# Norms of the first layer's weights over pairs of pieces, and four features at a time in one-tile chunks

## The chip, the cores and the metric

The kernel runs on one core of one Trainium2 chip. The metric is the device time of one execution in microseconds (us), lower is better. The engines are TensorE (PE, with its weight loads PEld), VectorE (DVE), ScalarE (ACT), GpSimd (POOL) and SyncE (SP), which issues the DMA transfers.

## What is computed

Attention within clusters, then two feed-forward layers. B = 2, H = 8 heads, S = 768, D = 64; 16 clusters; model width 512, hidden width 2048.

```
q_assign, k_assign = argmax over the centroids of the normalised q and k
mask  = q_assign[:, :, :, None] == k_assign[:, :, None, :]
x     = softmax(where(mask, q @ k.T / sqrt(D), -1e9)) @ v     # to (1536, 512)
h     = x @ moe_w_in;   x = (h * sigmoid(h)) @ moe_w_out      # first layer
h     = x @ moe2_w_in
out   = (max(h, 0) + alpha * min(h, 0)) @ moe2_w_out          # second layer
```

## The kernel before, in words

All data is fp32 and every product is made of three fp16 products: an operand x is scaled by a power of two and split into a high and a low fp16 part, and high x high, high x low and low x high are added in PSUM.

The tokens are 12 tiles of 128. Attention goes tile by tile and, in a tile, head by head; one head of one tile is a unit. `front` (L786) makes its scores on PE (L796, L800), the scaling and the maximum on DVE (L810), the exponential and its high part on ACT (L815, L819) and its low part on DVE (L820); a transposing DMA (L826) turns the result and `back` (L828) multiplies it with v (L838). When the eight heads of a tile are done, `x_done` (L851) scales and splits the tile of x and a DMA transposes it.

The first layer, `layer1` (L1158), takes tiles in chunks, `CHUNKS` (L22): chunks 0 and 1 have one tile each (n = 128 columns), the other five have two (n = 256). For each of the KF = 16 blocks of 128 hidden features it makes 12 matmuls (L1190). Two blocks share one PSUM tile `hp` of 2 x n columns, taken from the two banks `w` in turn (the function `psum`, L469). Then come four elementwise instructions over both blocks: tanh on ACT (L1197), a product on DVE (L1198), the high part on ACT (L1201) and the low part on DVE (L1202). The scale of tanh is a column of `dh`, which in chunk 0 is made one column at a time (L1180) as the scales of the weights arrive. After that, 4 output blocks of 48 matmuls each (L1221), evacuated by ACT (L1228).

The weights come as fp32 words in pieces of 128 x 1024: 8 pieces of `moe_w_in` (`in_tasks`, L958) and 8 of `moe_w_out` (`out_tasks`, L1008). A piece is loaded (L892), converted by ACT (L903, L907) and DVE (L914, L917), and its sum of squares is taken by `sum_sq_pe` (L946): 8 matmuls of 128 x 128 blocks of the piece with themselves, added in a `w` bank (L952), and one DVE instruction that takes the diagonal and adds it up (L954, with an accumulator read). `scale` (L981) sums over a pair of pieces and over the partitions with matmuls against ones (`all_sum`, L503), makes a power of two (`pow2_scale`: L445 and L447 on DVE, L450 and L453 on POOL) and splits both pieces (L929 on ACT, L930 on DVE); then the buffers of the pair are loaded again. Both columns of a pair get the same scale. For `moe_w_out` one scale over all 8 pieces is made (L1033) and the pieces are split after it. These functions serve the second layer's weights too; there (`w2`) the sum of squares is an ACT instruction (L944).

The program's order is not the order on the engines. `plan_order` (L313) gives all instructions a cost from a table in the code (`costs`, L75), finds their dependences, and lays them out on the engines' queues by a list schedule: once in program order, then 60 times backward and forward with priorities that carry Gaussian noise (`improve`, L193). The order with the earliest modelled end of all of these is then forced on the queues of PE, DVE, ACT, POOL and SP. Which PSUM bank a tile gets is fixed before, by the program's order.

Of the kernel before, what the change touches and what calls it, by code (L numbers as in the profile page):

```python
# [11 lines left out]
F32 = mybir.dt.float32  # L12
# [34 lines left out]
class Plan:  # L47
# [144 lines left out]

    def improve(self, rounds):  # L193

        noise = Random(1)
        found = [self.run(list(range(len(self.ins))))]
        back = self.mirror()
        for _ in range(rounds):
            back.run([noise.gauss(0, 0.1) - t for t in self.ended])
            found.append(self.run([noise.gauss(0, 0.1) - t for t in back.ended]))  # L200
        return min(found, key=lambda x: x[0])
# [128 lines left out]
def cluster_attention_silu_prelu(  # L330
# [20 lines left out]
    nc = tc.nc  # L351
# [25 lines left out]
    def view(off, dt, *dims):  # L377
        n = 1
        for d in dims:
            n *= d  # L380
        nb = n * (2 if dt in (F16, BF16) else 4)
        assert off % 4 == 0 and nb % 4 == 0 and off + nb <= total, (off, nb)
        a = arena[:, off // 4:(off + nb) // 4]
        if dt != F32:
            a = a.bitcast(dt)
        if len(dims) == 1:
            return a
        names = [f"a{i}" for i in range(len(dims))]
        pat = f"p ({' '.join(names)}) -> p {' '.join(names)}"
        return a.rearrange(pat, **{n: d for n, d in zip(names, dims)})  # L390
# [103 lines left out]
    def all_sum(cols, kind="m"):  # L494

        if not isinstance(cols[0], list):
            cols = [cols]
        n = cols[0][0].shape[1]
        ps = psum(kind, n * len(cols))
        for q, line in enumerate(cols):  # L500
            for i, c in enumerate(line):
                top = c.bitcast(BF16).rearrange("p (n t) -> p n t", t=2)[:, :, 1]
                nc.tensor.matmul(  # L503
                    out=ps[:, q * n:(q + 1) * n], lhsT=ones, rhs=top, start=(i == 0), stop=(i == len(line) - 1)
                )
        return ps
# [436 lines left out]

        nc.scalar.activation(out=junk, in_=t, func=ACTF.Square, accum_out=ss)  # L944

    def sum_sq_pe(tb, ss, kind):  # L946


        ps = psum(kind, 128)
        for i in range(PC // 128):  # L950
            c = tb[:, i * 128:(i + 1) * 128]
            nc.tensor.matmul(out=ps, lhsT=c, rhs=c, start=(i == 0), stop=(i == PC // 128 - 1))  # L952
        junk = view(o_junk, BF16, 128)
        nc.vector.scalar_tensor_tensor(  # L954
            out=junk, in0=ps, scalar=1.02, in1=ident, op0=ALU.mult, op1=ALU.mult, accum_out=ss
        )

    def in_tasks(w, raws, o_dst, kind, modes, mp):  # L958

        m = Weight()  # L960
        m.s, m.inv, ss = col(NPC), col(NPC), col(NPC)
        m.smin, m.inv_smin = col(1), col(1)
        tasks = []

        def raw(j):
            return view(raws[j % len(raws)], I32, PC, 2)

        def load(j):
            if j < NPC:
                n = w.shape[0] // 2  # L970
                return load_piece(w[j % 2 * n:(j % 2 + 1) * n, j // 2 * 2 * FW:(j // 2 + 1) * 2 * FW], raw(j))

        def conv(j):
            t = raw(j)[:, :, 1].bitcast(F32)
            to_f32(raw(j), t, mp[j])
            if w2:
                sum_sq(t, raw(j)[:, :, 0].bitcast(F32), ss[:, j:j + 1])
            else:
                sum_sq_pe(view(raws[j % len(raws)], BF16, PC, 4)[:, :, 3], ss[:, j:j + 1], kind)

        def scale(b):  # L981
            if not w2:
                for o in range(8 * b, 8 * b + 8):
                    assert o < 8 or (("k", 0, (o - 8) // 3) if o < 20 else ("v", 0, (o - 20) // 3)) in did
            both = range(2 * b, 2 * b + 2)
            tot = all_sum([[ss[:, j:j + 1] for j in both]] * 2, kind)
            pow2_scale(tot, 2, 14 if w2 else 15, None, m.s[:, both[0]:both[0] + 2], m.inv[:, both[0]:both[0] + 2])
            for j in both:
                d = view(o_dst + 8 * KB * b, F16, 2, 2, PC)[:, :, j % 2]
                t = raw(j)[:, :, 1].bitcast(F32)  # L990
                split(t, d[:, 0], d[:, 1], m.s[:, j:j + 1], modes[j])
            for j in both:
                load(j + len(raws))
            if b == NPC // 2 - 1:
                nc.vector.tensor_reduce(out=m.smin, in_=m.s, axis=AX.X, op=ALU.min)
                nc.vector.tensor_reduce(out=m.inv_smin, in_=m.inv, axis=AX.X, op=ALU.max)

        m.loads = [lambda j=j: load(j) for j in range(len(raws))]
        m.scales = [lambda b=b: scale(b) for b in range(NPC // 2)]
        for j in range(NPC + 1):  # L1000
            if j < NPC:
                tasks.append(lambda j=j: conv(j))
            if j and j % 2 == 0:
                tasks.append(m.scales[j // 2 - 1])
        m.tasks = tasks
        return m

    def out_tasks(w, raws, o_ts, o_dst, m_in, kind, modes, mp):  # L1008

        m = Weight()  # L1010
        s, m.inv, ss, rho = col(1), col(1), col(NPC), col(NPC)

        def raw(j):
            return view(raws[j % len(raws)], I32, PC, 2)

        def load(j):
            if j < NPC:
                n = w.shape[0] // NPC
                load_piece(w[j * n:(j + 1) * n], raw(j))

        def conv(j):
            if not w2 and j < 6:
                for o in range(4 * j, 4 * j + 4):
                    assert ("k", 0, o // 6) in did
            t = view(o_ts[j], F32, PC)
            to_f32(raw(j), t, mp[j])
            if w2:
                sum_sq(t, raw(j)[:, :, 0].bitcast(F32), ss[:, j:j + 1])
            load(j + len(raws))
            if not w2:  # L1030
                sum_sq_pe(view(o_ts[j], BF16, PC, 2)[:, :, 1], ss[:, j:j + 1], kind)

        def scale():  # L1033
            tot = all_sum([ss[:, j:j + 1] for j in range(NPC)], kind)
            pow2_scale(tot, 1, 15, None, s, m.inv)
            nc.vector.tensor_scalar(rho, m_in.inv, m_in.smin, s, op0=ALU.mult, op1=ALU.mult)

        def piece(j):
            d = out_piece(o_dst, j)
            split(view(o_ts[j], F32, 2, DM), d[:, 0], d[:, 1], rho[:, j:j + 1], modes[j])  # L1040

        m.loads = [lambda j=j: load(j) for j in range(len(raws))]
        m.tasks = [lambda j=j: conv(j) for j in range(NPC)]
        m.scale = scale
        m.late = [lambda j=j: piece(j) for j in range(NPC)]
        return m
# [111 lines left out]
    def layer1(c):  # L1158
# [14 lines left out]
        first = t0 % T == 0  # L1173
        if c and first:
            nc.vector.tensor_scalar(dh, w1["in"].inv, x_inv[b], 0.5, op0=ALU.mult, op1=ALU.mult)
        for f in range(KF):
            j = f // 2
            wi = [in_block(o_w, f // 2 * 2 + ff) for ff in range(2)]
            if c == 0 and f % 2 == 0:
                nc.vector.tensor_scalar(  # L1180
                    dh[:, j:j + 1], w1["in"].inv[:, j:j + 1], x_inv[b], 0.5,
                    op0=ALU.mult, op1=ALU.mult,
                )
            if f % 2:
                hp = psum("l", 2, n)
                for ff in range(2):
                    i = 0
                    for kd in range(KD):
                        for a, bb in ((0, 0), (0, 1), (1, 0)):
                            nc.tensor.matmul(  # L1190
                                out=hp[:, ff], lhsT=wi[ff][:, a, kd],
                                rhs=mov(bb, kd), start=(i == 0), stop=(i == 3 * KD - 1),
                            )
                            i += 1
                th = view(o_tmp + 2 * KB * ring("t1", 2), F32, 2, n)
                gh, gl = g[:, f - 1:f + 1, 0], g[:, f - 1:f + 1, 1]
                nc.scalar.activation(out=th, in_=hp, func=ACTF.Tanh, scale=dh[:, j:j + 1])  # L1197
                nc.vector.scalar_tensor_tensor(  # L1198
                    out=th, in0=th, scalar=1.0, in1=hp, op0=ALU.add, op1=ALU.mult
                )  # L1200
                nc.scalar.activation(out=gh, in_=th, func=ACTF.Copy, scale=2.0 ** -16)  # L1201
                nc.vector.scalar_tensor_tensor(  # L1202
                    out=gl, in0=th, scalar=2.0 ** -16, in1=gh, op0=ALU.mult, op1=ALU.subtract,
                )
            yield
# [395 lines left out]
```

## Time and profile before

| what | value |
|---|---|
| median of 3 runs (lowest to highest) | 753.65 us (753.04 to 754.53) |
| the profiled execution: time, span | 756.6 us, 754.8 us |
| PE busy | 663.7 us (88%) |
| DVE busy | 598.3 us (79%) |
| ACT busy | 482.2 us (64%) |
| POOL busy | 128.7 us (17%) |
| mean granted clock of TensorE | 0.964 |

The span is the part of the profiled execution that the trace covers; all times of rows are in us from its start, if not marked ns. Busy shares are means over stages with different limits, so they say little by themselves; the rows below go by stretches.

### The profile page before, as it was taken

The numbers are of one execution on the slowest core, as the hardware profiler recorded it, in microseconds if no ns is written. First come the engines' busy times: TensorE is split into PE (matmuls) and PEld (weight loads), VectorE is DVE, ScalarE is ACT, GpSimd is POOL, SyncE is SP. The second block draws the span as 40 slices with busy tenths as digits, with TensorE's granted clock in tenths as the row PEclk, the third lists the DMA queues.
The fourth block names the chain that finished last, engine by engine and source line by source line (L and its number), as shares of the span: only waits on it lengthen the run. The fifth ranks groups of instructions, "written<-read, shape, count | busy, mean of one in ns | idle before, by whom it ended". The sixth has DMA issues, their size and how long they took to land.

```text
span 754.8 us, 17044 instructions
## 1 busy us (share of the span) xinstructions
PE 663.7 (88%) x7035; PEld 500.2 (66%) x7035; DVE 598.3 (79%) x1084; ACT 482.2 (64%) x779; POOL 128.7 (17%) x231
## 2 busy tenths in 40 slices
PE   0363568689999999999999999998899999999997
PEld 0243346579888888888888898874344677666643
DVE  4798998998888689858977856779899999966650
ACT  7886967978879568747866967878664442422111
POOL 4442021432234532102120020100000000000000
PEclk9995558999999999999999999999999999999999
DMA  7979998999999898888897932353300100001001
GB/s 230 307 196 288 331 216 132 172 196 172 195 181 209 147 168 137 135 153 146 149 152 124 279 76 97 129 199 140 112 1 0 56 2 1 1 1 56 1 0 56
DMA packets 237357, 100.86 MB, mean 134 GB/s; under 512 B 217312, under 2 KB 227552, under 8 KB 237280
## 3 DMA queue, kind: packets, MB, share of 16 engines
q1 hardware_dynamic: 237280, 99.78, 60.9%
q8 instruction: 55, 0.90, 0.5%
q14 instruction: 22, 0.18, 0.1%
HBM read 43.03 MB, written 3.15 MB: 61 GB/s over the span
## 4 chain that ended last, share of the span: by engine, by line
PE 46%; DVE 13%; DMA 6%; ACT 4%; issue 3%; POOL 2%; ACTq 0%; POOLq 0%
PE s L1477 11%; PE w L1190 10%; PE w L1221 9%; PE x L838 4%; PE w L1434 4%; DVE arena L930 3%; DMA arena<-in_moe_w_out_dram 3%; PE s L796 2%; PE s L800 2%; DMA arena<-in_moe_w_in_dram 2%; PE x L1434 2%; PE m L1434 2%; DVE arena L1300 1%; DVE arena L917 1%; DVE arena L914 1%
## 5 line engine op out<-in xcount | busy, mean ns | idle before, releaser
L1190 PE MATMUL w<-arena 128*128 128x256 f16 (+1 forms) x1272 | 152.7, 258 | 3.6 <-DMA arena<-arena 2.3
L1221 PE MATMUL w<-arena 128*128 128x256 f16 (+1 forms) x1296 | 154.1, 257 | 1.6 <-DVE arena L1198 1.1
L1477 PE MATMUL s<-arena 128*128 128x512 f16 x576 | 136.1, 379 | 1.4 <-DVE arena L930 1.4
L838 PE MATMUL x<-arena 128*128 128x64 f16 x1728 | 120.3, 196 | 7.3 <-DMA arena<-arena 7.3
L1190 PEld LDWEIGHTS <-arena 128*128 128x128 f16 x1344 | 109.7, 98 | 18.3 <-issue 6.7
L1221 PEld LDWEIGHTS <-arena 128*128 128x128 f16 x1344 | 110.2, 98 | 16.2 <-issue 2.1
L815 ACT ACTIVATE s<-s,stat 128x768 f32<-128x768 f32 x96 | 83.9, 873 | 56.0 <-DVE s L810 49.2
L810 DVE TENSOR_SCALAR_CACHE_REDUCE s<-s,stat 128x768 f32<-128x768 f32 x96 | 97.6, 1021 | 24.3 <-PE s L800 23.2
L838 PEld LDWEIGHTS <-arena 128*128 128x128 f16 x1728 | 97.5, 100 | 19.7 <-DMA arena<-arena 9.3
L820 DVE TENSOR_TENSOR arena<-s,arena 128x768 f16<-128x768 f32 x96 | 91.4, 953 | 13.0 <-ACT arena L819 12.6
L1477 PEld LDWEIGHTS <-arena 128*128 128x128 f16 x576 | 56.0, 98 | 61.1 <-issue 2.3
L796 PE MATMUL s<-arena 80*128 80x384 f16 x192 | 68.0, 354 | 12.6 <-DVE arena L820 11.1
L819 ACT ACTIVATE arena<-s 128x768 f16<-128x768 f32 x96 | 77.5, 809 | 1.7 <-DMA arena<-arena 0.3
L1434 PEld LDWEIGHTS <-arena 128*128 128x128 f16 x672 | 65.6, 98 | 17.3 <-issue 1.0
L1394 ACT ACTIVATE arena<-arena,stat 128x512 f16<-128x512 f32 x48 | 33.6, 717 | 66.1 <-DVE arena L1391 66.0
L800 PE MATMUL s<-arena 128*128 128x384 f16 x192 | 68.2, 355 | 0.0
L450 POOL TENSOR_SCALAR stat<-stat 128x1 int32<-128x1 int32 (+1 forms) x41 | 11.6, 286 | 307.0 <-DVE stat L445 210.1
L914 DVE SCALAR_TENSOR_TENSOR arena<-arena 128x1024 int32<-128x1024 int32 x32 | 39.1, 1222 | 22.6 <-ACT arena L907 22.4
L1434 PE MATMUL w<-arena 128*128 128x256 f16 x336 | 56.5, 273 | 0.0
L930 DVE SCALAR_TENSOR_TENSOR arena<-arena,stat 128x1024 f16<-128x1024 f32 x40 | 51.9, 1315 | 4.9 <-ACT arena L929 4.9
L903 ACT ACTIVATE arena<-arena 128x1024 int32<-128x1024 uint32 x32 | 37.0, 1155 | 26.8 <-DMA arena<-in_moe_w_in_dram 16.4
L929 ACT ACTIVATE arena<-arena,stat 128x1024 f16<-128x1024 f32 x40 | 45.7, 1171 | 11.7 <-POOL stat L450 4.4
(176 smaller groups left out, 1061.6 us busy)
## 6 DMA issues: line engine op xcount, KB each, us to landing
arena<-in_moe_w_in_dram SPq DMA_DIRECT2D x16, 1024.0 KB, 6.1
arena<-in_moe_w_out_dram SPq DMA_DIRECT2D x16, 1024.0 KB, 6.4
arena<-in_k_dram SPq DMA_DIRECT2D x8, 384.0 KB, 4.8
arena<-in_q_dram SPq DMA_DIRECT2D x6, 512.0 KB, 5.1
arena<-in_v_dram SPq DMA_DIRECT2D x8, 384.0 KB, 5.1
out_dram<-arena SPq DMA_DIRECT2D x12, 256.0 KB, 2.1
arena<-arena SPq DMA_TRANSPOSE x149, 4.2
arena<-in_centroids_dram SPq DMA_DIRECT2D x1, 32.0 KB, 2.9
```

The costliest lines, as they stand in the source:

```text
L796: nc.tensor.matmul(out=sc[:, j, :hs], lhsT=qt2[0:D + C, h], rhs=kt2[0:D + C, h % 2, j * hs:(j + 1) * hs], start=True, stop=False,)
L800: nc.tensor.matmul(out=sc[:, j, :hs], lhsT=qt1[:, h], rhs=kt1[:, h % 2, j * hs:(j + 1) * hs], start=False, stop=True,)
L810: nc.vector.tensor_scalar(sc[:, :, :hs], sc[:, :, :hs], nd_cols[:, H * (n % 2) + h:H * (n % 2) + h + 1], None, op0=ALU.mult, op1=ALU.min, ...
L815: nc.scalar.activation(out=p, in_=p, func=ACTF.Exp, scale=-1.0, bias=bias, accum_out=sums[n % 2][:, h:h + 1])
L819: nc.scalar.activation(out=hl[:, 0], in_=p, func=ACTF.Copy)
L820: nc.vector.tensor_tensor(out=hl[:, 1], in0=p, in1=hl[:, 0], op=ALU.subtract)
L838: nc.tensor.matmul(out=x_ps[0][:, h], lhsT=pt[:, ph * T + t], rhs=vt[:, h % 2, t, vh], start=(i == 0), stop=(i == 3 * T - 1),)
L930: nc.vector.scalar_tensor_tensor(out=lo, in0=t, scalar=s, in1=hi, op0=ALU.mult, op1=ALU.subtract)
L1190: nc.tensor.matmul(out=hp[:, ff], lhsT=wi[ff][:, a, kd], rhs=mov(bb, kd), start=(i == 0), stop=(i == 3 * KD - 1),)
L1221: nc.tensor.matmul(out=acc, lhsT=wo[:, a, f % 2, dt * 128:(dt + 1) * 128], rhs=g[:, f, bb], start=(i == 0), stop=(i == 3 * KF - 1),)
L1434: nc.tensor.matmul(out=hp[:, ff], lhsT=a_[:, a, kd, at + 128 * ff:at + 128 * ff + 128], rhs=b_[:, bb, kd], start=(k == 0), stop=(k == 5),)
L1477: nc.tensor.matmul(out=acc[t], lhsT=g[:, q, a, t * 128:(t + 1) * 128], rhs=wo[:, bb, f % 2], start=(first and q == 0 and k == 0), stop=(la ...
```

## The change

`sum_sq_pe` takes a list of pieces: for the first layer's weights it is called once for each pair of pieces, after the odd one, and adds 16 matmuls in one bank before one reduction on DVE. The sum of squares of a pair stands in the odd piece's column, and the sums over the partitions read the odd columns alone. In `layer1`, `nf = 512 // n` blocks of features share a PSUM tile: four in the one-tile chunks, two in the others as before; the four elementwise instructions then go over 4 x 128 columns. `dh` is made for two columns at a time. The planner's random numbers start from 4 in place of 1.

```diff
     def improve(self, rounds):
-        noise = Random(1)
+        noise = Random(4)
...
-    def sum_sq_pe(tb, ss, kind):
+    def sum_sq_pe(tbs, ss, kind):
         ps = psum(kind, 128)
-        for i in range(PC // 128):
-            c = tb[:, i * 128:(i + 1) * 128]
-            nc.tensor.matmul(out=ps, lhsT=c, rhs=c, start=(i == 0), stop=(i == PC // 128 - 1))
+        parts = [tb[:, i * 128:(i + 1) * 128] for tb in tbs for i in range(PC // 128)]
+        for i, c in enumerate(parts):
+            nc.tensor.matmul(out=ps, lhsT=c, rhs=c, start=(i == 0), stop=(i == len(parts) - 1))
...
# in_tasks
-            else:
-                sum_sq_pe(view(raws[j % len(raws)], BF16, PC, 4)[:, :, 3], ss[:, j:j + 1], kind)
+            elif j % 2:
+                sum_sq_pe(
+                    [view(raws[i % len(raws)], BF16, PC, 4)[:, :, 3] for i in (j - 1, j)],
+                    ss[:, j:j + 1], kind,
+                )
...
-            tot = all_sum([[ss[:, j:j + 1] for j in both]] * 2, kind)
+            tot = all_sum([[ss[:, j:j + 1] for j in (both if w2 else both[1:])]] * 2, kind)
...
# out_tasks
-            if not w2:
-                sum_sq_pe(view(o_ts[j], BF16, PC, 2)[:, :, 1], ss[:, j:j + 1], kind)
+            if not w2 and j % 2:
+                sum_sq_pe(
+                    [view(o_ts[i], BF16, PC, 2)[:, :, 1] for i in (j - 1, j)],
+                    ss[:, j:j + 1], kind,
+                )
...
-            tot = all_sum([ss[:, j:j + 1] for j in range(NPC)], kind)
+            tot = all_sum([ss[:, j:j + 1] for j in range(0 if w2 else 1, NPC, 1 if w2 else 2)], kind)
...
# layer1
+        nf = 512 // n
         for f in range(KF):
-            j = f // 2
-            wi = [in_block(o_w, f // 2 * 2 + ff) for ff in range(2)]
-            if c == 0 and f % 2 == 0:
+            j = f // 4 * 2
+            if c == 0 and f % 4 == 0:
                 nc.vector.tensor_scalar(
-                    dh[:, j:j + 1], w1["in"].inv[:, j:j + 1], x_inv[b], 0.5,
+                    dh[:, j:j + 2], w1["in"].inv[:, j:j + 2], x_inv[b], 0.5,
                     op0=ALU.mult, op1=ALU.mult,
                 )
-            if f % 2:
-                hp = psum("l", 2, n)
-                for ff in range(2):
+            if f % nf == nf - 1:
+                hp = psum("l", nf, n)
+                for ff in range(nf):
                     i = 0
+                    wi = in_block(o_w, f - nf + 1 + ff)
...
-                                out=hp[:, ff], lhsT=wi[ff][:, a, kd],
+                                out=hp[:, ff], lhsT=wi[:, a, kd],
...
-                th = view(o_tmp + 2 * KB * ring("t1", 2), F32, 2, n)
-                gh, gl = g[:, f - 1:f + 1, 0], g[:, f - 1:f + 1, 1]
+                th = view(o_tmp + 2 * KB * ring("t1", 2), F32, nf, n)
+                gh, gl = g[:, f - nf + 1:f + 1, 0], g[:, f - nf + 1:f + 1, 1]
```

## Rows read from the trace of the kernel before

**Rows 1.** Busy time by stretch; columns: stretch, length, engines, PE clock, DMA share, GB/s.

```profile
20.00:125.00 105.00, 56.71 (x628) 41.42 (x629) 92.91 (x191) 80.48 (x111) 30.84 (x46) 0.74 1.00 255
125.00:200.00 75.00, 65.35 (x1191) 57.13 (x1188) 69.85 (x147) 64.66 (x126) 19.77 (x31) 1.00 1.03 172
200.00:460.00 260.00, 259.19 (x3373) 224.48 (x3371) 196.40 (x387) 186.57 (x329) 61.98 (x96) 1.00 0.86 160
460.00:620.00 160.00, 151.23 (x1002) 95.64 (x1001) 144.47 (x187) 105.19 (x147) 6.21 (x22) 1.00 0.22 80
620.00:755.00 135.00, 129.82 (x826) 80.30 (x824) 84.76 (x138) 31.87 (x47) 0.34 (x2) 1.00 0.05 16
```

**Rows 2.** Instructions by line and form: min/median/max ns with first, last start; or busy, mean ns.

```profile
L954 DVE SCALAR_TENSOR_TENSOR arena<-w,arena x16: 273/282/292, 25.5 to 124.4; 128x128 bf16<-128x128 f32 x16
L954 DVE DVE_READ_ACCUMULATOR arena<-w,arena x16: 75/83/85, 25.7 to 124.6; 128x1 f32 x16
...
L1180 DVE TENSOR_SCALAR stat<-stat x8: 196/199/202, 103.8 to 105.9; 128x1 f32<-128x1 f32 x8
...
L1197 ACT ACTIVATE arena<-w,stat x16: 465/474/492, 123.9 to 196.2; 128x256 f32<-128x256 f32 x16
...
L1198 DVE SCALAR_TENSOR_TENSOR arena<-arena,w x16: 408/414/422, 126.0 to 198.3; 128x256 f32<-128x256 f32 x16
...
L1202 DVE SCALAR_TENSOR_TENSOR arena<-arena x16: 409/418/427, 128.0 to 200.5; 128x256 f16<-128x256 f32 x16
...
L1202 DVE SCALAR_TENSOR_TENSOR arena<-arena 128x512 f16<-128x512 f32 x40 | 29.5, 739 | 4.2 <-ACT arena L1201 4.1
...
L1197 ACT ACTIVATE arena<-w,stat 128x512 f32<-128x512 f32 x37 | 25.3, 684 | 5.7 <-PE w L1190 5.3 <-DVE arena L1202 0.2
L1198 DVE SCALAR_TENSOR_TENSOR arena<-arena,w 128x512 f32<-128x512 f32 x37 | 25.2, 682 | 3.0 <-ACT arena L1197 3.0
L1201 ACT ACTIVATE arena<-arena 128x512 f16<-128x512 f32 x40 | 24.9, 626 | 2.2 <-DVE arena L1198 1.9
...
L1201 ACT ACTIVATE arena<-arena 128x256 f16<-128x256 f32 x16 | 6.6, 414 | 1.5 <-DVE arena L1198 1.3
```

**Rows 3.** Timeline of DVE: start, duration (us), line, operation, shapes, count.

```profile
47.10 0.28 DVE L954 SCALAR_TENSOR_TENSOR arena<-w,arena 128x128 bf16<-128x128 f32 x1
...
47.31 1.22 DVE L917 SCALAR_TENSOR_TENSOR arena<-arena 128x1024 int32<-128x1024 int32 x1
...
103.81 0.56 DVE L1180 TENSOR_SCALAR stat<-stat 128x1 f32<-128x1 f32 x4
...
152.51 0.41 DVE L1198 SCALAR_TENSOR_TENSOR arena<-arena,w 128x256 f32<-128x256 f32 x1
152.85 0.42 DVE L1202 SCALAR_TENSOR_TENSOR arena<-arena 128x256 f16<-128x256 f32 x1
153.18 1.02 DVE L810 TENSOR_SCALAR_CACHE_REDUCE s<-s,stat 128x768 f32<-128x768 f32 x1
...
231.53 0.68 DVE L1198 SCALAR_TENSOR_TENSOR arena<-arena,w 128x512 f32<-128x512 f32 x1
232.13 0.68 DVE L1202 SCALAR_TENSOR_TENSOR arena<-arena 128x512 f16<-128x512 f32 x1
```

**Rows 4.** Waits from 20 to 125 us, then 125 to 200: total us, times, longest.

```profile
PE w L952 <- DVE arena L917: 14.0, 5, 5.6
PE w L952 <- DVE arena L954: 3.0, 3, 1.0
...
ACT arena L903 <- DMA arena<-in_moe_w_in_dram: 7.8, 3, 4.8
...
PE x L838 <- DMA arena<-arena: 5.2, 5, 2.5
PE w L1190 <- DVE arena L1198: 1.3, 3, 0.7
...
PE w L1221 <- DVE arena L1198: 1.1, 1, 1.1
```

## Prediction

> **What bounds the kernel now.** I read first the busy time of each engine by stretches of the span [rows 1]. There the reader is to see a change of limit. From 200 to 460 us TensorE (PE) is busy 259.2 of 260 us, and from 200 to the end it idles 0.8 + 8.8 + 5.2 = 14.8 us in all. So nothing done to VectorE (DVE) or ScalarE (ACT) there can give more than part of 14.8 us. Before 200 us PE is far from full: 56.7 of 105 us from 20 to 125, 65.4 of 75 from 125 to 200. In the same stretches DVE is busy 92.9 of 105 (88%) and 69.9 of 75 (93%), ACT 77% and 86%. The DMA engines show a share of 1.00 and 1.03. The early part is therefore carried by DVE, with transfers close behind, and whatever brings PE sooner to its full load moves everything after 200 us forward by the same amount.
>
> Second, the instructions of the lines that the diff touches, with their first and last start [rows 2]. All lie before 201 us: the 16 norm reductions (L954) from 25.5 to 124.4 us, the eight dh products from 103.8 to 105.9, the elementwise work of the two one-tile chunks from 123.9 (its first tanh, L1197) to 200.5. Third, the timeline of DVE [rows 3], for the distance from the start of one instruction to the start of the next, since durations overlap. Last, the waits in the two early stretches [rows 4].
>
> **The change, part by part.** The sum is made against the profiled execution: 756.6 us with a span of 754.8, so 1.8 us lie around the span. It is 2.95 us above the median of the three runs (753.65), and I take that off at the end.
>
> *Norms over pairs.* The number of norm matmuls (L952) stays at 128. Of the 16 reductions with their accumulator reads 8 go. By duration one is 0.282 + 0.083 us, together 8 x 0.365 = 2.9 us [rows 2]. In the timeline the next real instruction starts 0.21 us after the reduction (47.10 to 47.31) [rows 3], so DVE gets back 8 x 0.21 = 1.7 us. The sums over partitions (L503) lose 2 matmuls in each of 4 scales and 4 in the last: 12 one-column matmuls on a PE that idles half of that stretch, costed at nothing; were PE full there they would be a gain of some tenths. A norm group now opens with the even piece and closes with the odd one, so one of the two w banks is held from the first to the last of 16 matmuls. Before, a scale waited for the odd piece too, so the scale (L445, L450), the split (L929, L930) and the next weight load behind it get no later. PE's three waits of a norm for a reduction before it, 3.0 us [rows 4], go, since only one bank is now taken per pair; what is late next is the conversion itself (L917), for which PE waits 14.0 us [rows 4], so those 3.0 us count for nothing. If the order puts the even piece's matmuls too early, the score matmuls (L796, L800) queue behind them on PE; a DVE instruction needs those soon, and the longest of these waits is now 5.6 us [rows 4].
>
> *dh in four steps instead of eight.* Four in a row take 0.56 us with 0.199 for one [rows 2, 3], so (0.56 - 0.20)/3 = 0.12 us apart: 4 x 0.12 = 0.5 us saved. That a second column costs nothing is an assumption; the bound is the same price twice, which gives no saving.
>
> *Elementwise work over four features.* 16 instructions of 256 columns become 8 of 512 in each of four lines. L1198: the next instruction starts 0.34 us after the 256-column form (152.51 to 152.85) and 0.60 after the 512-column one (231.53 to 232.13) [rows 3]: 16 x 0.34 - 8 x 0.60 = 0.6. L1202: 0.33 us apart (152.85 to 153.18) for 256 columns; for 512 I take the same 0.60, as its duration in that place is L1198's 0.68 [rows 3]: 16 x 0.33 - 8 x 0.60 = 0.5. ACT by duration: L1197 16 x 0.474 - 8 x 0.684 = 2.1 and L1201 16 x 0.414 - 8 x 0.626 = 1.6 [rows 2]; ACT has 10 us free in 125 to 200 [rows 1], so its 3.7 us stand at nothing, covered by DVE; without that cover they would be a further gain.
>
> DVE's sum is 1.7 + 0.5 + 0.6 + 0.5 = 3.3 us, of which 2.2 lie before 125 us and 1.1 behind. Weighted with DVE's busy share (for in the rest of the time another thing ended the wait) 2.2 x 0.88 + 1.1 x 0.93 = 3.0 us.
>
> By full durations the same four terms are 2.9 + 0.8 + (16 x 0.414 - 8 x 0.682 = 1.2) + (16 x 0.418 - 8 x 0.739 = 0.8) = 5.7 us [rows 2]. In the timeline DVE's instructions start 0.07 to 0.09 us before the one ahead has ended [rows 3], so 3.3 is what I take, and 5.7 is an end of the range. The Trainium skill ("VectorE: DVE Perf Modes", The DRAIN you can't avoid) says that the next op does not start until the pipe is empty, with an exception for ops that are not held; by that rule the sum would be the 5.7. This trace speaks for the exception: its starts lie closer than its durations.
>
> *What it adds.* A 512-column group passes tanh and L1198 (0.684 + 0.682) in place of 0.474 + 0.414, so the last group of a chunk releases its bank and gives its g 0.48 us later. The output matmuls (L1221) already wait once, 1.1 us, for L1198 [rows 4], and nothing but attention's own matmuls lies behind them on PE. Two chunks x 0.48 is 1.0 us at most, nothing at least; attention covers part, and I take 0.5.
>
> *The order.* The planner's random start is another (4 in place of 1), and its list of instructions is another, so every engine's queue can differ over the whole span. No row shows a second order. The nearest rows are single waits that an order can make or spare: 5.6 us for a conversion, 4.8 us for a weight load [rows 4]. So I bound it at 5 us either way and take 0, because every term above has a place in the trace and this one has none. No DMA is added or taken away and none moves in the program; where SP's queue puts them belongs to the same unknown.
>
> Net: 3.0 - 0.5 = 2.5 us. 756.6 - 2.5 = 754.1 for the profiled kind of run, less 2.95: **751.2 us**. About 0.2% of this kernel (1.5 us) is what a measurement can tell from no change.
>
> **The rivals.** *Transfers set the early stretch, and DVE's gain is hidden.* For it: a DMA share of 1.00 and 1.03 [rows 1], ACT's 7.8 us of waits for weight loads and PE's 5.2 us for transposes [rows 4]. Against it: the waits with the most microseconds, 14.0, are for DVE. Only some 0.3 us would come through: 753.4 us.
>
> *The banks are held longer and PE waits in the one-tile chunks (slower).* The place is L1190 from 120 to 200 us, with two banks for groups of 48 matmuls. PE now waits three times for L1198, 1.3 us, 0.7 the longest [rows 4]. If each of the eight groups waited 0.7 us, that is 5.6 us; with the gain of 3.0 the net is +2.6: 756.3 us. It decides once the time from a group's last matmul to the end of its L1198 is longer than the other bank's group and the attention work put beside it. For it: in that stretch DVE is 93% busy [rows 1], so L1198 stands in a queue. Against it: PE spends twice as long on each bank, which gives that queue twice the time.
>
> *The new order is better by one such stall.* The place is the 48 us in which PE idles from 20 to 125 us [rows 1]. It spares 5 us more: 746.2 us.
>
> *The new order is worse by one such stall.* It gives back 5 us: 756.2 us. For both there is only that they are possible; a list with 8 reductions and 32 elementwise instructions less leaves the planner a little more room, so the better one gets the larger chance.
>
> **How the numbers follow.** Forecast 0.46, better order 0.16, hidden 0.20, banks 0.10, worse order 0.08. Faster by over 0.2% takes the forecast and the better order: 0.62. Within 0.2%: hidden, 0.20. Slower: banks and worse order, 0.18. The forecast's own range goes from 748 (savings by full durations, 756.6 - 5.7 - 2.95) to 752.7 (a third of DVE's gain lost and 1.0 us paid at the chunk ends: 756.6 - 2.0 + 1.0 - 2.95). The range over the cases goes from 746.0, which takes in the better order, to 756.0, which takes in the hidden case and stops just short of the two slower ones.
>
> **What would show it.** In the profile after: L954 8 times with its duration unchanged, L1180 4 times, L1197 to L1202 8 times at 128x512 where 256 stood; DVE's busy time down by about 5.7 us in all; PE's full stretch beginning some 2 to 3 us sooner; busy time of PE unchanged but for the clock. The bank rival shows as waits of L1190 for L1198 of several us in 120 to 200. The hidden case shows as the same start of chunk 0 (its first tanh is at 123.9 us now) with more DVE idle. The forecast is wrong if chunk 0 begins more than 3 us sooner or later than now by waits that no touched line takes part in, or if the difference arises after 200 us: then the order made it.

## The result, and the profile after

The changed kernel takes 744.38 us (median of 4 runs, 743.56 to 746.65) against 753.35 us for the kernel before on the same chip: ratio 0.9864, 95% interval 0.9837 to 0.9892. That is 9.0 us less, where 2.5 had been forecast, and the time lies under the range of the forecast. The profiled execution has a span of 742.9 us, 11.9 under the one before.

Line numbers move by two to five: the norm matmuls are L950 and their reduction L952 (L952 and L954 before), the first-layer matmuls L1195 (L1190), the four elementwise lines L1202, L1203, L1206 and L1207 (L1197 to L1202), the output matmuls L1226 (L1221).

First the page's line of busy times, then busy time by stretch of the changed kernel, the same stretches and columns as [rows 1]:

```profile
PE 661.5 (89%) x7023; PEld 500.3 (67%) x7023; DVE 596.1 (80%) x1048; ACT 480.3 (65%) x763; POOL 123.9 (17%) x231
```

```profile
20.00:125.00 105.00, 59.01 (x680) 43.97 (x681) 94.65 (x185) 83.35 (x117) 32.14 (x48) 0.76 1.05 257
125.00:200.00 75.00, 69.16 (x1247) 62.14 (x1245) 66.91 (x122) 61.14 (x109) 17.51 (x30) 0.98 0.99 175
200.00:460.00 260.00, 257.44 (x3307) 222.04 (x3305) 201.88 (x392) 193.01 (x335) 59.91 (x98) 1.00 0.89 161
460.00:620.00 160.00, 156.36 (x1019) 97.59 (x1018) 149.74 (x199) 100.92 (x140) 4.40 (x20) 1.00 0.20 76
620.00:743.00 123.00, 118.12 (x756) 73.36 (x753) 72.97 (x118) 28.46 (x43) 0.34 (x2) 1.00 0.05 18
```

PE's idle time is what the reader is to compare. From 20 to 200 us it was 57.9 us [rows 1] and is 51.8: 6.1 us less. From 460 to 620 it was 8.8 and is 3.6: 5.1 less, in a stretch that holds no line of the diff; from 200 to 460 it grew from 0.8 to 2.6. PE's busy time fell from 663.7 to 661.5, 2.2 us, and PE idles 0.2 less from 620 us on. 6.1 + 5.1 - 1.8 + 2.2 + 0.2 gives the 11.9 us of the span, but for rounding. So about half of the gain lies in the stretch that the forecast spoke of and a good quarter, 5.1 - 1.8, behind 200 us, where the diff changes nothing but the order of the queues and when their work begins.

DVE's busy time fell by 2.2 us (598.3 to 596.1), ACT's by 1.9. The instructions themselves are as forecast, in the view by line up to 215 us: 8 norm reductions of the duration that [rows 2] has for 16, 4 products for `dh` (L1184) with 222 ns in place of 199, and elementwise lines at 512 columns. The counts of 11 and 10 take in the first groups of chunk 2.

```profile
L952 DVE SCALAR_TENSOR_TENSOR arena<-w,arena x8: 278/283/292, 26.4 to 122.1; 128x128 bf16<-128x128 f32 x8
L952 DVE DVE_READ_ACCUMULATOR arena<-w,arena x8: 77/82/84, 26.6 to 122.3; 128x1 f32 x8
...
L1184 DVE TENSOR_SCALAR stat<-stat x4: 218/222/223, 75.2 to 85.9; 128x2 f32<-128x2 f32 x4
...
L1202 ACT ACTIVATE arena<-w,stat x11: 677/687/697, 122.8 to 214.0; 128x512 f32<-128x512 f32 x11
...
L1203 DVE SCALAR_TENSOR_TENSOR arena<-arena,w x11: 635/677/689, 123.8 to 214.7; 128x512 f32<-128x512 f32 x11
...
L1207 DVE SCALAR_TENSOR_TENSOR arena<-arena x10: 678/682/1154, 125.9 to 212.6; 128x512 f16<-128x512 f32 x10
```

The waits of PE from 20 to 125 us and from 125 to 200, as in [rows 4]:

```profile
PE w L950 <- DVE arena L917: 18.9, 9, 5.6
PE x L838 <- DMA arena<-arena: 8.6, 6, 3.0
...
PE x L838 <- DMA arena<-arena: 3.8, 2, 3.2
...
PE w L1195 <- DVE arena L1203: 0.5, 1, 0.5
PE w L1226 <- DVE arena L930: 0.4, 1, 0.4
```

The wait of a norm for the reduction before it (3.0 us) is gone, but the wait of the norms for the conversion grew from 14.0 to 18.9 us, so those 3.0 brought nothing by themselves, as forecast. The wait of the first layer's matmuls for their bank fell from 1.3 to 0.5 us: larger groups did not lengthen it. What moved is when the one-tile chunks get done. Here are the output matmuls of chunks 0 and 1, 384 in all, by stretches (columns: stretch, length, PE, PEld, clock, DMA share, GB/s), first before (L1221), then after (L1226):

```profile
140.00:160.00 20.00, 2.35 (x24) 1.67 (x25) 1.00 1.06 197
160.00:180.00 20.00, 10.52 (x155) 9.23 (x154) 1.00 1.16 195
180.00:200.00 20.00, 3.75 (x53) 3.16 (x54) 1.00 1.08 176
200.00:215.00 15.00, 10.46 (x143) 8.50 (x140) 1.00 1.10 199
```

```profile
140.00:160.00 20.00, 8.36 (x102) 7.26 (x100) 0.91 1.11 198
160.00:180.00 20.00, 5.40 (x72) 4.23 (x68) 1.00 1.06 174
180.00:200.00 20.00, 13.61 (x190) 11.75 (x190) 1.00 0.95 176
200.00:215.00 15.00, 0.60 (x5) 0.20 (x3) 1.00 1.04 175
```

143 of them ran after 200 us before the change and 5 after it. By the timeline of PE the last one ends at 214.7 us before and at 201.4 after. From 200 to 460 us PE is full in both kernels (idle 0.8 and 2.6 us), so work done earlier, in time that was idle, is time won.

### The profile page after: what moved, and what is told of

The parts are those of the page before. It is cut to its first block, busy times and chain, and to the rows that moved or that the text cites. A ratio compares the mean times of both kernels' runs of the same rounds, so it can differ in the third digit from the quotient of the medians.

```text
span 742.9 us, 16966 instructions
## 1 busy us (share of the span) xinstructions
PE 661.5 (89%) x7023; PEld 500.3 (67%) x7023; DVE 596.1 (80%) x1048; ACT 480.3 (65%) x763; POOL 123.9 (17%) x231
## 4 chain that ended last, share of the span: by engine, by line
PE 43%; DVE 13%; DMA 6%; ACT 5%; issue 4%; POOL 2%; ACTq 0%; POOLq 0%; DVEq 0%
PE s L1482 11%; PE w L1195 9%; PE w L1226 7%; PE w L1439 4%; PE x L838 3%; DVE arena L930 3%; PE m L1439 2%; PE x L1439 2%; DMA arena<-in_moe_w_out_dram 2%; PE s L800 2%; PE s L796 2%; DMA arena<-in_moe_w_in_dram 2%; DMA arena<-arena 1%; DVE arena L917 1%; DVE arena L1305 1%
## 5 line engine op out<-in xcount | busy, mean ns | idle before, releaser
L1226 PE MATMUL w<-arena 128*128 128x256 f16 (+1 forms) x1296 | 154.8, 258 | 1.2 <-ACT arena L1233 0.9
L1195 PE MATMUL w<-arena 128*128 128x256 f16 (+1 forms) x1272 | 147.6, 256 | 1.0 <-DMA arena<-arena 0.5
L1482 PE MATMUL s<-arena 128*128 128x512 f16 x576 | 132.1, 379 | 1.7 <-DVE arena L930 1.3
L838 PE MATMUL x<-arena 128*128 128x64 f16 x1728 | 117.5, 197 | 13.3 <-DMA arena<-arena 13.3
L1226 PEld LDWEIGHTS <-arena 128*128 128x128 f16 x1344 | 111.6, 99 | 14.7 <-issue 1.4
L1195 PEld LDWEIGHTS <-arena 128*128 128x128 f16 x1344 | 110.8, 98 | 14.8 <-issue 2.0
L1399 ACT ACTIVATE arena<-arena,stat 128x512 f16<-128x512 f32 x48 | 33.9, 718 | 67.5 <-DVE arena L1396 67.4
L930 DVE SCALAR_TENSOR_TENSOR arena<-arena,stat 128x1024 f16<-128x1024 f32 x40 | 50.9, 1289 | 8.8 <-ACT arena L929 8.8
L1439 PE MATMUL w<-arena 128*128 128x256 f16 x336 | 52.0, 273 | 0.0
L903 ACT ACTIVATE arena<-arena 128x1024 int32<-128x1024 uint32 x32 | 36.8, 1149 | 21.9 <-DMA arena<-in_moe_w_out_dram 11.8
```

Of the source, the lines that this page charges most:

```text
L838: nc.tensor.matmul(out=x_ps[0][:, h], lhsT=pt[:, ph * T + t], rhs=vt[:, h % 2, t, vh], start=(i == 0), stop=(i == 3 * T - 1),)
L930: nc.vector.scalar_tensor_tensor(out=lo, in0=t, scalar=s, in1=hi, op0=ALU.mult, op1=ALU.subtract)
L1195: nc.tensor.matmul(out=hp[:, ff], lhsT=wi[:, a, kd], rhs=mov(bb, kd), start=(i == 0), stop=(i == 3 * KD - 1),)
L1226: nc.tensor.matmul(out=acc, lhsT=wo[:, a, f % 2, dt * 128:(dt + 1) * 128], rhs=g[:, f, bb], start=(i == 0), stop=(i == 3 * KF - 1),)
L1439: nc.tensor.matmul(out=hp[:, ff], lhsT=a_[:, a, kd, at + 128 * ff:at + 128 * ff + 128], rhs=b_[:, bb, kd], start=(k == 0), stop=(k == 5),)
L1482: nc.tensor.matmul(out=acc[t], lhsT=g[:, q, a, t * 128:(t + 1) * 128], rhs=wo[:, bb, f % 2], start=(first and q == 0 and k == 0), stop=(la ...
```

## The experiments

Three theories stood at the start. **A**: the parts give the 2.5 us of the forecast and the new order the rest. **B**: the parts give all. **C**: every program and every random start draws an order of its own, and one draw tells little of the parts. Eighteen kernels were run. For each the table has the ratio to the kernel before with its interval and four readings of its trace (us): when the scale of `moe_w_out` is applied (`rho`, the last line of `scale` in `out_tasks`), when the last output matmul of chunks 0 and 1 ends, PE's idle time before 200 us, and that from 200 to 620. The planner deals its random numbers out instruction by instruction, so the same start in two programs does not make the same order; pairs of equal starts are set side by side below only to have as many draws of one program as of the other.

| kernel, random start | ratio (interval) | rho | chunks end | idle to 200 | idle 200 to 620 |
|---|---|---|---|---|---|
| before, 1 | 1 | 126.8 | 214.7 | 76.5 | 9.6 |
| before, 2 | 1.0039 (1.0020 to 1.0058) | 129.1 | 211.8 | 73.8 | 10.8 |
| before, 3 | 1.0009 (0.9992 to 1.0026) | 128.2 | 211.2 | 75.0 | 11.8 |
| before, 4 | 1.0030 (1.0009 to 1.0050) | 124.3 | 214.1 | 75.2 | 11.0 |
| changed, 1 | 0.9936 (0.9910 to 0.9962) | 118.7 | 200.9 | 71.0 | 12.2 |
| changed, 2 | 0.9965 (0.9939 to 0.9991) | 119.4 | 199.6 | 67.0 | 13.5 |
| changed, 3 | 0.9875 (0.9849 to 0.9901) | 118.3 | 196.6 | 67.5 | 9.8 |
| changed, 4 | 0.9864 (0.9837 to 0.9892) | 124.4 | 201.4 | 70.4 | 6.2 |
| norms alone, 4 | 1.0033 (1.0010 to 1.0055) | 143.3 | 211.7 | 79.3 | 10.1 |
| features alone, 4 | 0.9969 (0.9949 to 0.9989) | 136.5 | 213.5 | 73.3 | 8.0 |
| norms, banks apart, 4 | 1.0018 (1.0001 to 1.0034) | 119.2 | 208.0 | 70.6 | 11.2 |
| norms, banks apart, 1 | 0.9940 (0.9917 to 0.9962) | 119.8 | 206.1 | 68.3 | 9.9 |
| features, banks apart, 4 | 0.9933 (0.9905 to 0.9962) | 121.1 | 199.9 | 70.7 | 8.6 |
| features, banks apart, 1 | 0.9979 (0.9957 to 1.0002) | 126.8 | 203.9 | 73.6 | 10.8 |
| changed, banks shared, 4 | 0.9974 (0.9954 to 0.9993) | 139.1 | 206.2 | 72.9 | 8.7 |
| changed, banks shared, 3 | 0.9969 (0.9948 to 0.9991) | 139.2 | 210.5 | 71.6 | 10.3 |
| changed, banks shared, 1 | 0.9983 (0.9961 to 1.0005) | 137.8 | 205.9 | 72.4 | 11.1 |
| changed, norms in bank m, 4 | 0.9980 (0.9962 to 0.9998) | 139.6 | 203.9 | 71.1 | 11.4 |
| changed, in halves, 4 | 0.9976 (0.9962 to 0.9990) | 119.4 | 205.1 | 71.8 | 12.1 |
| changed, in halves, 3 | 0.9980 (0.9952 to 1.0008) | 117.6 | 201.9 | 70.3 | 11.6 |

### The order: other random starts

The edit is one number, in the changed kernel (first line of the diff) and in the kernel before (second); starts 2 and 3 likewise in both:

```diff
-        noise = Random(4)
+        noise = Random(1)
...
-        noise = Random(1)
+        noise = Random(4)
```

> The whole change, but with the planner's random start left at 1. Theory A (the code's parts give the 2.5 us of the prediction, the new order the other 6 to 7): about 751 us. Theory B (the parts give all of the 9 us, the order nothing): about 744 us. Theory C (each program and each random start draws an order of its own, and one draw tells little of the parts): anything from 743 to 757.

> The kernel before with the random start 4 and nothing else changed: the same instructions in another order. Theory A: about 747 us, the order's share alone. Theory B: 753.5 us, no change. Theory C: anything from 747 to 760, and not the difference that the start makes in the changed kernel.

> The whole change with random start 2. So far start 4 gave 0.986 of the kernel before and start 1 gave 0.994. If the parts have a worth of their own that no order takes away, this one lies under the kernel before too, at 0.985 to 0.997. If the order alone decides (theory C), it can lie above 1 as well.

> The same with random start 3: 0.985 to 0.997 if the parts have a worth of their own, anything from 0.985 to 1.01 if the order alone decides.

> The kernel before with random start 2, another draw of its order: 0.997 to 1.006 if orders of one program differ by some 0.3%, as start 4 did (1.003); under 0.99 if an order alone can bring what the change brought.

> The kernel before with random start 3: as with start 2, 0.997 to 1.006 if orders of one program differ by some 0.3%, under 0.99 if an order alone can bring 9 us.

The changed kernel with start 1 gave 0.9936, which is 748.5 us on the scale of the first comparison and lies between the 751 of theory A and the 744 of theory B. The kernel before with start 4 gave 1.0030: start 4 by itself brings nothing, it makes the kernel before slightly slower. All four draws of the changed kernel lie under all four of the kernel before. With the same start the differences are 0.64, 0.74, 1.34 and 1.66%; the mean is 1.10%, 8.3 us. The draws of one program differ too, by 1% in the changed kernel, so this mean has a standard error of some 0.26%, 2 us. Without the two draws that the kernels came with (start 1 before, start 4 after) it is 1.01%, 7.6 us. So the diff is worth about 8 us, give or take 2 by that standard error; the 2.5 of theory A lies nearly three of these errors away, and theory A falls. Theory C is right in part: one draw tells the worth to 3 or 4 us only.

The two halves of the span behave differently here: the end of chunks 0 and 1 comes at 197 to 201 us in every draw of the changed kernel and at 211 to 215 in every one of the kernel before, while the idle time from 200 to 620 us runs from 6.2 to 13.5 in the former and from 9.6 to 11.8 in the latter. On the means of the four traces the span is 9.8 us shorter; PE's idle time before 200 us is 6.2 less, that from 200 to 620 only 0.3 less, and PE's busy time 3.3 less, the cause of which stays open. So the early part is where the diff pays in every draw, and start 4 happened to have the best late part of the four.

### Each part alone

Norms over pairs alone keep the old loop of `layer1`; features alone keep a norm for each piece. Both with start 4.

```diff
# norms alone, against the changed kernel
-            if f % nf == nf - 1:
-                hp = psum("l", nf, n)
+            if f % 2:
+                hp = psum("l", 2, n)
...
# features alone, against the changed kernel
-            elif j % 2:
-                sum_sq_pe(
-                    [view(raws[i % len(raws)], BF16, PC, 4)[:, :, 3] for i in (j - 1, j)],
-                    ss[:, j:j + 1], kind,
-                )
+            else:
+                sum_sq_pe(view(raws[j % len(raws)], BF16, PC, 4)[:, :, 3], ss[:, j:j + 1], kind)
```

> Norms over pairs alone (one-tile chunks in pairs of features as before), random start 4. Theory A: 1.5 us under the kernel before with start 4, so about 745.5 us. Theory B: between 744.4 and 753.4, by the share of this part. Theory C: within 5 us of 750, with no sum of parts that comes out.

> Four features at a time in the one-tile chunks alone (a norm for each piece as before), random start 4. Theory A: 1 us under the kernel before with start 4, about 746 us. Theory B: between 744.4 and 753.4, the rest of the 9 us after the norms' share. Theory C: within 5 us of 750, with no sum of parts that comes out.

Against the kernel before with the same start (1.0030) the norms gave nothing (1.0033) and the features 0.6% (0.9969); together they give 1.66%. These are single draws, and no sum of the parts comes out of them, as theory C had it; but the trace shows something that the parts do to each other. The scale of `moe_w_out`, applied at 124.3 us in the kernel before with start 4, is late in both. The two answers are of norms alone and features alone, the first start being that of this weight:

```profile
L1040 DVE TENSOR_SCALAR stat<-stat x2: 281/282/284, 143.3 to 552.1; 128x8 f32<-128x8 f32 x2
```

```profile
L1036 DVE TENSOR_SCALAR stat<-stat x2: 280/284/289, 136.5 to 546.0; 128x8 f32<-128x8 f32 x2
```

The reason that suggests itself is in the program's order. While chunk 0 is written down, one conversion of `moe_w_out` is put ahead of each second feature step, and norms and groups take the two w banks in turn. Before the change the sequence is norm, group, norm, group: all norms fall on one bank and all groups on the other. With both parts it is again one norm for one group. With either part alone it is one norm for two groups, or two norms for one, and the turn no longer separates them. The banks of PE's matmuls in the order of its queue, from the compiled programs (n a norm of `moe_w_out`, G a group of chunk 0; the banks are called 68 and 69):

```
before           n68 (8 norms)          G69 G69 G69 G69 G69 G69 G69 G69
changed          n68 (4 norms)          G69 G69 G69 G69
norms alone      n69 G68 G69 G68 n68 G69 G68 n69 G68/G69 n68
features alone   n68 n69 n69 G68 G69 n68 n68 G68 n69 n69 n68 G69
```

Where they share banks, a norm has to come after a group that needs tile 0 of x, the scale waits for the norm, and the splits of `moe_w_out` (L930), on which every output matmul depends, wait for the scale. That is theory **D**.

### The banks kept apart, or shared on purpose

Kept apart: the norms of `moe_w_out` (the call in `out_tasks`) name one w bank and the groups of chunk 0 the other, and the ring is turned as before. The lines stand here as norms alone has them, the last pair as features alone has it (in norms alone it names `"w1"` with 2 in place of `nf`).

```diff
-        elif kind == "w":
-            t = bank_w[ring("w", 2)]
+        elif kind[0] == "w":
+            i = ring("w", 2)
+            t = bank_w[int(kind[1:] or i)]
...
-                    ss[:, j:j + 1], kind,
+                    ss[:, j:j + 1], "w0",
...
-                hp = psum("l", nf, n)
+                hp = psum("l" if c else "w1", nf, n)
```

Shared: the whole change with one more turn of the ring after each group of chunk 0. No instruction is added.

```diff
                 hp = psum("l", nf, n)
+                if c == 0:
+                    ring("w", 2)
```

> Norms over pairs alone, and the two w banks dealt out as they fall in the whole change: the second weight's norms in one, chunk 0's groups in the other. Theory D (each part alone flips the turn of the two banks, so that norms of the second weight wait for groups of chunk 0, which eats its gain): rho comes before 127 us instead of at 143, chunks 0 and 1 end before 205 us instead of at 209, and the time is 0.5 to 1% under norms alone (758.3), near 0.993 of the kernel before. Theory C (an order is a draw): rho and the end of the chunks stay where they were, 1.000 to 1.004.

> Four features at a time alone, with the same fixed banks. Theory D: rho before 129 us instead of at 136.5, chunks 0 and 1 ended by about 203 us instead of 212, 0.988 to 0.994 of the kernel before. Theory C: as before, 0.994 to 1.000.

> The whole change with one more turn of the two banks after each group of chunk 0, so that norms and groups share both banks; no instruction is added. Theory D: the norms wait for groups, rho moves from 124 to 135 us or later, chunks 0 and 1 end at 207 us or later instead of 200, and the time goes back to 0.995 to 1.002 of the kernel before. Theory B' (the 8 us come from the instructions saved, wherever the tiles lie): it stays at 0.985 to 0.990.

> The whole change with both banks shared by norms and groups, random start 3 (the whole change with that start: 0.9875). Theory D: rho at 134 us or later instead of 118, chunks 0 and 1 ended at 203 to 208 us instead of 196, 0.993 to 1.002. Theory C: the result with start 4 was a draw, and this one can lie at 0.9875 or under it.

> The same with random start 1 (the whole change with that start: 0.9936, chunks ended at 198 us). Theory D: rho at 134 us or later instead of 119, chunks ended at 203 to 208 us, 0.996 to 1.004. Theory C: no sign in the difference.

> Norms over pairs alone with the banks kept apart, random start 1. Theory D: rho at 118 to 124 us, chunks 0 and 1 ended at 203 to 207 us, TensorE idle before 200 us near 71 us as with start 4 (75 on the mean of the kernel before); the whole time 0.993 to 1.002, by the late stage. Theory C: idle of 73 to 77 us.

> Four features at a time alone with the banks kept apart, random start 1. Theory D: rho at 120 to 126 us, chunks 0 and 1 ended at 198 to 203 us, TensorE idle before 200 us near 71 us; the whole time 0.988 to 0.998. Theory C: chunks ended anywhere up to 212 us.

With the banks shared the changed kernel goes from 0.9864 to 0.9974, from 0.9875 to 0.9969 and from 0.9936 to 0.9983: 1.10, 0.94 and 0.47%, some 6 us on the mean, in three draws and with the same instructions. Start 2, whose changed kernel was the slowest draw with 0.9965, was not tried; against the mean of all four draws of the changed kernel the loss is 0.65%, 5 us. The scale moved from 124.4 to 139.1 us in the first of them:

```profile
L1040 DVE TENSOR_SCALAR stat<-stat x2: 283/432/582, 139.1 to 542.0; 128x8 f32<-128x8 f32 x2
```

Rho comes after 137 us in all three and the chunks end 5 to 14 us later (206.2 with start 4, where 207 or later was expected, and 210.5 with start 3, where 208 at most was). That the bank is what holds the norms back can be seen on PE. These are the norm matmuls (L950) by stretches, first of the changed kernel, then with shared banks and start 1 (columns as in the table of output matmuls). The last conversion (L917) ends at 117.1 us in both, and with shared banks the conversions of the second pair had ended at 95.2:

```profile
105.00:120.00 15.00, 3.99 (x31) 3.08 (x31) 0.68 1.08 217
120.00:135.00 15.00, 0.22 (x1) 0.10 (x1) 1.00 0.73 125
```

```profile
105.00:120.00 15.00, 0.00 (x0) 0.00 (x0) 0.67 1.02 208
120.00:135.00 15.00, 3.96 (x48) 3.18 (x48) 1.00 0.76 143
```

Three of the four norms stand behind groups of chunk 0, though their pieces were there. So theory D holds for the scale and for the end of the chunks; what it costs in the whole time is known to a few us.

With the banks apart the parts alone bring rho to 119 to 127 us and the end of the chunks to 206 to 208 (norms) and 200 to 204 (features). Norms with start 4 miss their mark of 205 us, and their time, 1.0018, lies where theory C had put it and not near 0.993, for the late part with 11.2 us of idle gave something back; features with start 1 miss three marks narrowly (rho 126.8, the end of the chunks 203.9, 73.6 us of idle before 200 us where 71 was expected). The whole times scatter: norms 0.12 and 0.60% under the kernel before of the same start, 2.7 us on the mean; features 0.97 and 0.21%, 4.4 us. The sum, 7.1 us, is near the 8.3 of the whole. With draws of one program that scatter by 0.5%, means of two are good to some 3 us only.

### The norms in bank m

The edit is in `out_tasks`, and likewise in its sum over partitions:

```diff
-                    ss[:, j:j + 1], kind,
+                    ss[:, j:j + 1], "m",
```

> The whole change, with the second weight's norms and their sum in bank m, so that chunk 0's groups have both w banks in turn and wait for no norm. If one bank for the groups still costs something, chunk 0 ends sooner and the time is 0.98 to 0.986; if attention's small tiles in bank m now wait for the norms, the heads of tile 0 and 1 come later and it is 0.99 to 1.0.

0.9980, no better than with shared banks. Bank m takes attention's small tiles in turn, and here it is the norms that wait: rho is at 139.6 us. The heads did not come late (tile 0's x is scaled at 103.9 us, with 102.7 in the changed kernel), so the expectation named the wrong side of that coupling. Chunk 0's groups, with two banks in turn, were done early, at 132.6 us by the timeline, and it did not help. This is one draw.

### As many instructions as before, as few handovers as after

Chunk 0's groups hand over a single bank seven times before the change and three times after it. Whether this (theory **E**) or the fixed cost of each instruction (theory **F**) makes the worth of the features part, was asked by keeping four features in a bank and issuing the elementwise work in halves of 256 columns:

```diff
-                nc.scalar.activation(out=th, in_=hp, func=ACTF.Tanh, scale=dh[:, j:j + 1])
+                for h0 in range(0, nf, 2):
+                    hq, th = hp[:, h0:h0 + 2], th4[:, h0:h0 + 2]
+                    nc.scalar.activation(out=th, in_=hq, func=ACTF.Tanh, scale=dh[:, j:j + 1])
...
```

> The whole change, but tanh, L1203, L1206 and L1207 go over two features at a time again, 16 instructions of 256 columns per line, with four features still in a bank. Theory E (fewer handovers of the one bank): chunk 0's groups end at 137 to 143 us, chunks 0 and 1 at 198 to 202, and the time stays at 0.985 to 0.991. Theory F (the fixed cost of the instructions): chunk 0's groups end at 147 us or later, chunks 0 and 1 at 204 to 206, and the time goes to 0.994 to 1.002, where the norms alone lie.

> The same with random start 3. Theory E: 0.985 to 0.992, chunks 0 and 1 ended at 195 to 201 us. Theory F: 0.994 to 1.002, ended at 204 to 206.

0.9976 and 0.9980 against 0.9864 and 0.9875 for the same starts: 1.1%, 8 us, is lost twice, and what is left is what norms with the banks apart gave (0.9979 on the mean). By the time, theory F holds. But starts 4 and 3 are the two best of the changed kernel's four; against the mean of the four the loss is 0.68%, 5 us. Chunk 0's groups end at 148.9 and 146.2 us (138.9 and 139.3 in the changed kernel), as F wants for the first and nearly for the second; chunks 0 and 1 end at 205.1, as F wants, and at 201.9, between the two theories. Both draws also have 12 us of idle in the late part, where the changed kernel has 6.2 and 9.8, so of the 8 us lost some 2 to 6 lie there.

## Why the prediction was wrong

**What bounds the kernel** held. The early part is DVE's, PE is full from 200 us, and time won early moved the rest. The hidden case falls: chunks 0 and 1 end 13 us sooner with the transfers as they were (a DMA share of 1.05 and 0.99). The sign that the order made a difference, one that arises after 200 us, showed for some 3 of the 11.9 us of the span.

**The rival of the banks** falls: L1195 waits 0.5 us for its bank, not more than before. But the forecast spoke of two banks for the groups of chunk 0. They have one, before and after the change, since norms and groups alternate in the program's order; the buffers' numbers are not in the rows, and the order of the program was not counted through. That the change keeps this separation, while half of it would have lost it, is worth some 5 or 6 us that no row of the kernel before shows.

**The step that failed is the size of the parts' sum**: "3.0 - 0.5 = 2.5 us", worked out from distances between starts on DVE, with "ACT by duration ... its 3.7 us stand at nothing, covered by DVE". The runs put 8.3 us in its place, on the mean of four draws of each program. The distances were right for what they measure, the occupation of the engine: DVE's busy time fell by 3.4 us on the mean of the four draws (2.2 in the first pair), which is the 3.3 of that sum and not the 5.7 that were expected of the profile. ACT's fell by 0.9 (1.9 in the first pair) where the sum by duration had 3.7. So the time that DVE was occupied less was taken for the time that the kernel gains, and it gains more.

Why it gains more stays open in part. One reading is that engine time is not what counts here. The norm stands in a chain (L917, L950, L952, L503, the scale, L930), and tanh, L1203, L1206 and L1207 stand in one that changes engines at each step, ACT, DVE, ACT, DVE. By this reading an instruction in such a chain costs its whole duration, on either engine. By durations the terms on record were 2.9 + 0.8 + 1.2 + 0.8 on DVE and 2.1 + 1.6 on ACT, 9.4 us in all, within the error of the 8.3 measured. By part it is 2.9 for the norms, measured 2.7, and 6.5 for the features, measured 4.4; the distances give 1.5 for each. With an error of 3 us on each part, neither reading can be excluded there. The runs in halves put back 32 instructions, 2.0 us on DVE and 3.7 on ACT by these durations, and lost 8 us against equal starts and 5 against the mean. That the durations add up in this way is not shown: it was not tried by itself, by lengthening an instruction on ACT alone for example. A planner that finds better orders for fewer instructions would fit the whole times too, and no run separates the two.

**The 0.5 us at the ends of the chunks** can't be found: the output matmuls no longer wait for L1203, 1.1 us before [rows 4], and wait 0.4 us for a split instead.

**The order** was bounded rightly at 5 us either way (the four draws of the changed kernel lie 3.5 us under to 4.1 us above their mean), and its sign was open: start 4 has a late part with 3.4 us less of idle than the kernel before, and 4 to 7 less than the other three draws of the changed kernel. With start 1 or 2 the same diff would have given 0.9936 or 0.9965, 748.5 or 750.7 us, both inside the range; with start 3 it would have given 743.9, outside it. So the miss of the range is the parts' size and a good draw together.

The rule of the Trainium skill that was weighed ("VectorE: DVE Perf Modes", The DRAIN you can't avoid) would have put DVE's saving at 5.7 us. DVE's busy time, down by 3.4 us on the mean of four draws, speaks against that as the saving of occupation here, and for the exception that the Trainium skill makes in the same place.

## What to carry to other kernels

Price a saved instruction twice: by the distance of starts for an engine that is full, and by its whole duration, on every engine of the chain, where its result is waited for. Here the two were 3.0 and 9.4 us, and the measured worth lay near the larger one; where they differ so, the range has to hold both. Where tiles take PSUM banks in turn, count through the turns before and after a change to how many tiles there are: a part that saves instructions can lose its gain by making a tile wait for a bank of an unrelated chain, and then parts tried one at a time mislead. Where a planner with a random start orders the queues, run several starts of both programs before a difference under 1% is put down to the code, and compare with the mean of the starts and not with the best one.

## What was not expected of the hardware

The profile's busy time of DVE counts overlapping instructions once. The durations of all DVE instructions add up to 671.4 us in the trace before and 664.3 in the one after, 7.1 less (5.9 on the means of four draws); the busy time fell by 2.2 (3.4 on the means). The instruction behind a 512-column one starts 0.60 us after it, while its duration is 0.67 or 0.68, in the changed kernel as before [rows 3]. The timeline of DVE (start, duration, line):

```profile
128.90 0.67 DVE L1203 SCALAR_TENSOR_TENSOR arena<-arena,w 128x512 f32<-128x512 f32 x1
129.50 1.27 DVE L930 SCALAR_TENSOR_TENSOR arena<-arena,stat 128x1024 f16<-128x1024 f32 x1
```
